# Top-k attention feeding a PReLU MLP on one core: three pairs instead of four alternate at the end, and the MLP's steps are issued by another rule

## The chip, the cores and the metric

The kernel runs on one core of a Trainium2 chip. The core has five engines that work at the same time, each through its own queue of instructions in the order in which the program gives them: TensorE (PE in the profile, with its weight loads as PEld), VectorE (DVE), ScalarE (ACT), GpSimd (POOL) and SyncE (SP), which here only issues transfers. The metric is the device time of one execution in microseconds; the figure given for a kernel is the median of its runs.

## The reference

```
B, H, S, D = 8, 8, 576, 64                      # q, k, v
scores = q @ k.T / sqrt(D)
kth    = 32nd largest score of each row
attn   = softmax(where(scores >= kth, scores, -1e9))
x      = (attn @ v) with the heads side by side  # 4608 tokens x 512
h      = x @ w_in                                # 512 x 2048
g      = max(h, 0) + alpha * min(h, 0)
out    = g @ w_out                               # 2048 x 512
```

There are 64 heads, taken as 32 pairs. A pair has 2 x 576 rows of 576 scores, cut into nine tiles of 128 rows: two for each of four row blocks, and a ninth with the last 64 rows of both heads. So there are 288 tiles.

The PReLU is split. Since g = alpha h + (1 - alpha) max(h, 0), the output is x (w_in diag(alpha) w_out) + relu(x w_in) (diag(1 - alpha) w_out). The matrix in the first bracket, 512 x 512, is made once on the chip (`w_id`); it is called the linear matrix below.

## The kernel before, in words

All the work is written out by hand in one Python loop over ticks, n = 0 to 311, and each engine's queue is the order in which that loop emits. A tick handles one tile at each station of a pipeline:

- PE computes the scores of tile n+1 (`scores`, L314), for two tiles at once where a unit has two.
- ACT copies them out of PSUM with a per-row offset added (`act_b`, L323: tile b), counts signs (`act_s`, L329) and takes exponentials (`act_e`, L334).
- DVE forms the keys of tile n-1 (`flip`, L345: y), the eight largest of each of six segments of tile n-2 (L355: C), and merges those of tile n-3 (L370, L372). For every three tiles it picks the limit of each row, and seven ticks after a tile's scores it makes the mask (`mask`, L419). GpSimd multiplies mask and exponentials (L429). For the last six tiles DVE does both in one instruction (L426).
- SP issues a transposing transfer of the weights (wT<-w, L442), and PE multiplies them with v (`av`, L488: pu). DVE takes reciprocals (L505) and ACT scales the result into xb (`av_out`, L517).

Each pair is prepared before its first tile: transposes of q and k on PE, copies on ACT, row statistics through PE (pq, pk, pt, pg, pr, st in L175 to L240) and eight small steps on DVE. `prep_plan` gives each step a tick relative to `BASE[p]`, from 14 ticks before it to 2 before it. BASE is 9p for the first 28 pairs. The PSUM bank of pq, pk, pt and pg (tag "pa", one buffer) is shared by all pairs.

Of pairs 0 to 27 the nine tiles follow each other. The last batch (pairs P0 = 28 to 31, from tick N0 = 252) is ordered by row block instead: two tiles of each of the four pairs, then the four ninth tiles, then blocks 1, 2 and 3. So a row block of the output has its x before the whole batch is through. `av_last`, `rz_last` and `out_last` (L521 to L543) serve these, two pairs at a time, and DVE scales instead of ACT. BASE of the last four pairs is N0-5, N0-2, N0+2, N0+6.

The MLP is a list of steps, `back`. Each step has a part for PE, a part for ACT that empties the PSUM bank (or none), and a cost. The steps of a batch are added when its x has been turned by a transfer (`x_turn`, L551: xT<-xb): the transfers are issued at the end of tick n+7 and the steps are added at the end of n+8, n being the tick in which the batch's last weights are made. A block of 512 tokens has 16 steps of x w_in (`ph_step`, 4 matmuls each, cost 0.9, emptied by the relu at L641) and 4 x 3 steps of the second product (`pz_step`, 7, 7 and 6 matmuls, cost 1.5, emptied at L658 after the third). A block of 128 tokens has 4 and 3 steps. Weight preparation runs through the same list at the start, and its last four steps are the linear matrix, 16 matmuls each (L596), emptied at L600.

Before tick 252 one step is issued per tick, after that tick's scores; its ACT part is emitted in the next tick ahead of `act_b`. From tick 252 on a credit of 1.9 per tick (2.4 from tick 288) is spent by the cost of the steps, with several in a tick. Then the ACT part of a step is emitted just before the next step, in the same tick. In a tick the steps come on PE ahead of the preparation and the products with v.

## Time and profile before

| | |
|---|---|
| median of 3 runs | 928.11 us (926.97 to 928.45) |
| the profiled execution's own time | 929.21 us |
| its span, first to last instruction | 927.4 us |
| PE, DVE, ACT, POOL busy | 81%, 91%, 87%, 46% |
| mean granted TensorE clock | 0.908 |

The profile is of one execution. An engine's busy time is the time in which it has an instruction running. The rows of a view of groups or of time give line, engine, operation, the tile written and the tiles read, and a count; brackets at the end give the idle time before it and what ended it. The rows of the view by stretches give, for each stretch of time, the busy time of the five engines with the number of their instructions, the granted clock of TensorE (1 is full speed), the busy share of the transfer engines and what they moved. The rows of the view of waits say which instruction waited for which, in total, how often, and the longest.

### The profile page before, as it was taken

What the parts mean: (1) busy time and instruction counts of PE and PEld (TensorE: products, weight loads), DVE (VectorE), ACT (ScalarE), POOL (GpSimd) and SP (SyncE); (2) the same over time, 40 slices, a digit from 0 to 9 for tenths busy, and PEclk for the clock granted to TensorE, in tenths of its full rate; (3) what the DMA queues carried; (4) which work ended last, traced back from release to release, by engine and by line L of the source; (5) the groups of instructions that cost most, each with busy time, mean ns of one, the idle gap of its engine ahead of it and who ended that gap; (6) DMA issues with size and microseconds to landing.
All of it is one profiled execution on the core that took longest, in us unless ns stands there. A gap on an engine that the chain in (4) does not pass through costs nothing.

```text
span 927.4 us, 20789 instructions
## 1 busy us (share of the span) xinstructions
PE 752.0 (81%) x5702; PEld 448.4 (48%) x5779; DVE 847.7 (91%) x5305; ACT 810.4 (87%) x1873; POOL 431.0 (46%) x629
## 2 busy tenths in 40 slices
PE   5866797678977788878986889787986788989996
PEld 3544444344543445544553455544553444544564
DVE  3899969999999999999999999999999888999970
ACT  4999979799897999999897998999997988879842
POOL 0364534544554455555555454555554434455510
PEclk9565788799997999999977999999987999979999
DMA  6699634544556555564546546464456843353551
GB/s 149 121 174 200 132 65 86 105 93 91 124 106 111 92 103 110 115 115 93 126 99 124 95 88 126 97 125 94 106 126 103 146 85 74 76 101 62 115 94 45
DMA packets 343021, 99.52 MB, mean 107 GB/s; under 512 B 335200, under 2 KB 335216, under 8 KB 342896
## 3 DMA queue, kind: packets, MB, share of 16 engines
q1 hardware_dynamic: 340544, 95.71, 52.5%
q0 software_dynamic: 1152, 2.10, 1.6%
q8 instruction: 48, 0.79, 0.4%
q14 instruction: 77, 0.63, 0.2%
q10 hardware_dynamic: 1200, 0.30, 0.2%
HBM read 36.71 MB, written 9.44 MB: 50 GB/s over the span
## 4 chain that ended last, share of the span: by engine, by line
ACT 42%; PE 26%; DVE 24%; issue 3%; DMA 2%; POOL 1%; SPq 1%; ACTq 0%
ACT b L323 10%; ACT h L329 9%; ACT e L334 8%; DVE C L355 7%; PE ps L314 7%; PE pz L653 7%; PE ph L635 5%; ACT gT L641 4%; DVE mk L419 4%; DVE y L345 4%; DVE C L372 3%; DVE L L370 3%; ACT xb L517 2%; PE pz L649 2%; PE pg L206 2%
## 5 line engine op out<-in xcount | busy, mean ns | idle before, releaser
L429 POOL TENSOR_TENSOR w<-mk,e 128x576 bf16<-128x576 bf16 x250 | 319.2, 1277 | 375.3 <-DVE mk L419 208.3
L355 DVE MAX8 C<-y 128x8 f32<-128x96 f32 x1728 | 421.1, 244 | 0.1
L314 PE MATMUL ps<-qkT 64*128 64x288 f32 (+1 forms) x1280 | 255.9, 478 | 26.3 <-ACT b L323 26.1
L323 ACT ACTIVATE b<-ps,NT 128x576 f32<-128x576 f32 x288 | 201.5, 755 | 3.2 <-PE ps L314 3.2
L329 ACT ACTIVATE h<-b 128x576 bf16<-128x576 f32 x288 | 202.0, 701 | 2.0
L635 PE MATMUL ph<-xT,w_in_b 128*128 128x128 bf16 (+1 forms) x920 | 151.5, 302 | 54.4 <-ACT gT L641 27.2
L314 PEld LDWEIGHTS ps<-qkT 64*128 64x128 f32 (+1 forms) x1280 | 135.4, 195 | 86.4 <-ACT b L323 46.7
L334 ACT ACTIVATE e<-b 128x1152 bf16<-128x1152 f32 (+1 forms) x158 | 173.8, 1100 | 0.0
L370 DVE MAX8 L<-C 128x8 f32<-128x48 f32 x864 | 163.8, 190 | 0.1
L345 DVE TENSOR_SCALAR y<-b,SG 128x576 int32<-128x576 int32 x288 | 147.5, 512 | 10.0 <-POOL SG L339 9.4
L419 DVE TENSOR_SCALAR mk<-b,KP 128x576 bf16<-128x576 f32 x282 | 143.8, 510 | 0.0
L653 PE MATMUL pz<-w_out_b,gT 128*128 128x512 bf16 x551 | 134.2, 379 | 4.1 <-issue 3.0
L635 PEld LDWEIGHTS <-w_in_b 128*128 128x128 bf16 x960 | 70.8, 99 | 124.0 <-issue 93.9
L641 ACT ACTIVATE gT<-ph 128x512 bf16<-128x512 f32 x144 | 87.8, 618 | 41.8 <-PE ph L635 41.7
L372 DVE MATCH_REPLACE8 C<-L,C 128x48 f32<-128x48 f32 x576 | 109.1, 189 | 0.0
L653 PEld LDWEIGHTS <-gT 128*128 128x128 bf16 x576 | 52.7, 98 | 68.6 <-issue 13.1
L488 PE MATMUL pu<-v_bf,wT 128*128 128x65 bf16 (+1 forms) x1600 | 71.0, 201 | 11.0 <-DMA wT<-w 8.4
L339 POOL TENSOR_SCALAR SG<-S_all 128x1 int32<-128x1 f32 x288 | 65.2, 227 | 27.8 <-ACT h L329 27.5
L488 PEld LDWEIGHTS <-wT 128*128 128x128 bf16 (+1 forms) x1600 | 66.2, 105 | 24.6 <-DMA wT<-w 8.9
L429 POOL TENSOR_TENSOR wm<-mk,e 128x576 bf16<-128x576 bf16 x32 | 40.8, 1276 | 49.7 <-DVE mk L419 47.9
L329 ACT ACTIVATION_READ_ACCUMULATOR h<-b 128x1 f32 x288 | 61.6, 214 | 0.0
L658 ACT COPY o_sb<-pz 128x512 f32<-128x512 f32 x36 | 21.3, 591 | 39.4 <-PE pz L653 39.4
(102 smaller groups left out, 838.0 us busy)
## 6 DMA issues: line engine op xcount, KB each, us to landing
out_dram<-o_sb SPq DMA_DIRECT2D x35, 256.0 KB, 2.2
st_q<-in_q_dram SPq DMA_DIRECT2D x64, 128.0 KB, 2.9
st_v<-in_v_dram SPq DMA_DIRECT2D x64, 128.0 KB, 2.6
kst<-in_k_dram SPq DMA_DIRECT2D x62, 128.0 KB, 2.8
w_stage<-in_moe_w_out_dram SPq DMA_DIRECT2D x16, 256.0 KB, 3.1
w_in_b<-in_moe_w_in_dram POOLq DMA_DIRECT2D x8, 256.0 KB, 6.8
wT<-w SPq DMA_TRANSPOSE x128, 3.3
st_q<-in_q_dram SPq DMA_DIRECT2D x32, 32.0 KB, 2.8
```

What stands on the lines that cost most here:

```text
L314: nc.tensor.matmul(o_, l_, r_, start=True, stop=True)
L323: nc.scalar.activation(t["b"].rearrange("p (a c) -> p a c", a=2), t["ps"], AF.Identity, bias=NT0[:, p * TPP + j:p * TPP + j + 1], scale=ON ...
L329: nc.scalar.activation(h, tiles[n]["b"], AF.Sign, accum_out=S_all[:, n:n + 1])
L334: nc.scalar.activation(e, tiles[n0]["bu"], AF.Exp, scale=scl)
L345: nc.vector.tensor_scalar(t["y"].bitcast(I32), t["b"].bitcast(I32), FLIP, SG[:, n:n + 1], ALU.bitwise_xor, ALU.bitwise_xor)
L355: return [lambda g=g: nc.vector.max(out=C[:, n % TPP, g, :], in_=t["y"][:, g * SEG:(g + 1) * SEG]) for g in range(NSEG)]
L370: ops.append(lambda r=r, src=src: nc.vector.max(out=L[:, 8 * r:8 * r + 8], in_=src))
L419: nc.vector.tensor_scalar(t["mk"], t["b"], row_limit(n), None, ALU.is_ge)
L429: nc.gpsimd.tensor_tensor(dst, t["mk"], t["e"], ALU.mult)
L488: nc.tensor.matmul(o_, wT[:, 4 * side + c, cs], d["v"][:, 5 * side + c, :], start=(c == 0), stop=(c == 4))
L635: nc.tensor.matmul(hold[f][:, i, :], w_in_b[:, kk, (f + i) * 128:(f + i + 1) * 128], xT[:, kk, c0:c0 + tb], start=(kk == 0), stop=(kk == N ...
L653: nc.tensor.matmul(pz[0:m], hold["gT"][:, f, r0:r0 + m], w_out_b[:, f, :], start=False, stop=(f == NFT - 1))
```

## The change

1. Only the last three pairs (29, 30, 31; `LASTP`) alternate by row block. Pair 28 goes through its nine tiles like the pairs ahead of it, with `av` and `av_out`. `av_last` and its helpers take pairs 29 and 30 together and pair 31 alone.
2. BASE of the last four pairs is N0-3, N0+2, N0+7, N0+12: each five after the one before. Their first tiles come at N0, N0+9, N0+11 and N0+13.
3. The steps of a batch are added at the end of tick n+9 instead of n+8.
4. The linear matrix is made in twelve steps, of 6, 6 and 4 matmuls, instead of four of 16. One PSUM bank is held over the three.
5. ACT parts go into a queue that is emptied at the start of the next tick, throughout. A step that opens a PSUM bank ("takes") is not issued while `nb` parts are queued: 1 before tick BASE[31]-10 = 254, then 2. The second bank, shared with the preparation, opens to the MLP at tick 254 instead of 250.
6. The credit is used from the start. Several steps may be issued in a tick from N0-30 = 222 on instead of from 252.

```diff
-    ORDER += [(P0 + s, h) for s in range(KPB) for h in range(2)]
-    ORDER += [(P0 + s, 8) for s in range(KPB)]
-    ORDER += [(P0 + s, 2 * i + h) for i in range(1, 4) for s in range(KPB) for h in range(2)]
+    ORDER += [(P0, j) for j in range(TPP)]
+    LASTP = range(P0 + 1, NPAIR)
+    ORDER += [(p, h) for p in LASTP for h in range(2)]
+    ORDER += [(p, 8) for p in LASTP]
+    ORDER += [(p, 2 * i + h) for i in range(1, 4) for p in LASTP for h in range(2)]
...
-        m = 1 if n < N0 and ORDER[n][1] == 8 else 2
+        m = 1 if ORDER[n][1] == 8 and ORDER[n + 1][1] != 8 else 2
...
-    BASE.update({P0: N0 - 5, P0 + 1: N0 - 2, P0 + 2: N0 + 2, P0 + 3: N0 + 6})
+    BASE.update({P0: N0 - 3, P0 + 1: N0 + 2, P0 + 2: N0 + 7, P0 + 3: N0 + 12})
...
-        pul[i, g] = pu = ps_d.tile([128, 4, V1], FP32, name="pu", tag="pd")
-        for s in range(2):
-            d = pairs[P0 + 2 * g + s]
+        pul[i, g] = pu = ps_d.tile([128, 4 - 2 * g, V1], FP32, name="pu", tag="pd")
+        for s in range(2 - g):
+            d = pairs[P0 + 1 + 2 * g + s]
...
-        def w_id(kk):
-            hold["pl"] = pl = ps_m.tile([128, DM], FP32, name="pl", tag="misc")
-            for f in range(NFT):
+        def w_id(kk, part):
+            if part == 0:
+                hold["pl"] = ps_m.tile([128, DM], FP32, name="pl", tag="misc")
+            pl = hold["pl"]
+            for f in range(6 * part, min(6 * part + 6, NFT)):
...
-            if wp < P0:
+            if wp <= P0:
...
-                        put(n + 8, "end", lambda: feed((b + 1) * S))
-            elif (wj == 8 or wj % 2) and wp % 2:
-                i, g = (wj // 2, (wp - P0) // 2)
+                        put(n + 9, "end", lambda: feed((b + 1) * S))
+            elif (wj == 8 or wj % 2) and wp > P0 + 1:
+                i, g = (wj // 2, wp - P0 - 2)
...
-            banks[0] = 2 if n >= NT else 1 if n >= N0 - 2 else 0
+            banks[0] = 2 if n >= NT else 1 if n >= BASE[NPAIR - 1] - 10 else 0
...
-            if after:
-                after()
-            after = None
+            while after:
+                after.popleft()()
...
-            credit = min(credit, 0.0) + (2.4 if n >= NT else PE_TICK if n >= N0 else 0.0)
-            first = n < N0
-            while back and (first or credit > 0.0):
+            nb = 1 if n < BASE[NPAIR - 1] - 10 else 2
+            credit = min(credit, 0.0) + (2.4 if n >= NT else 1.9)
+            first = True
+            while back and credit > 0.0 and (first or n >= N0 - 30):
+                pe_f, act_f, cost, takes = back[0]
+                if takes and len(after) >= nb:
+                    break
+                back.popleft()
+                pe_f()
+                if act_f:
+                    after.append(act_f)
+                credit -= cost
                 first = False
-                if after:
-                    after()
-                pe_f, after, cost = back.popleft()
-                pe_f()
-                credit -= cost if n >= N0 else 0.0
```

More of the change, by code (lines that the diff above doesn't have):

```diff
@@ L610, in weight_steps @@
         for kk in range(NKT):
-            yield (lambda kk=kk: w_id(kk)), (lambda kk=kk: w_id2(kk))
+            for part in range(3):
+                yield ((lambda kk=kk, part=part: w_id(kk, part)),
+                       (lambda kk=kk: w_id2(kk)) if part == 2 else None)
     banks = [0, 0]
@@ L671, in mlp_steps @@
                 yield ((lambda r0=r0, m=m, part=part: pz_step(r0, m, part)),
-                       (lambda r0=r0, m=m: pz_act(r0, m)) if part == 2 else None, 1.5)
+                       (lambda r0=r0, m=m: pz_act(r0, m)) if part == 2 else None, 1.5, part == 0)
     blocks = []
@@ L744 @@
         scores(0)
-        back = deque((a, c, 1.0) for a, c in weight_steps())
+        back = deque((a, c, 1.0, 0) for a, c in weight_steps())
         credit = 0.0
-        after = None
+        after = deque()
         wdue, held = {}, []
@@ L759 @@
                     load_v(p)
-            banks[0] = 2 if n >= NT else 1 if n >= N0 - 2 else 0
+            banks[0] = 2 if n >= NT else 1 if n >= BASE[NPAIR - 1] - 10 else 0
             if n + 1 < NT and unit_of[n + 1][2] == 0:
                 scores(n + 1)
-            if after:
-                after()
-            after = None
+            while after:
+                after.popleft()()
             if n < NT:
```

11 lines of the change are left out of this document (6 added, 5 removed).

## The prediction

> **What bounds the kernel now.** I read the busy times on the page, then the view by stretches, then who waited for whom on DVE.
>
> ```profile
> PE 752.0 (81%) x5702; PEld 448.4 (48%) x5779; DVE 847.7 (91%) x5305; ACT 810.4 (87%) x1873; POOL 431.0 (46%) x629
> ```
> ```profile
> 400.00:600.00 200.00, 167.26 (x1310) 99.31 (x1327) 197.45 (x1242) 187.31 (x445) 101.72 (x143) 0.94 0.54 106
> ...
> 100.00:121.00 21.00, 13.82 (x100) 9.38 (x100) 21.00 (x136) 21.00 (x51) 11.57 (x17) 0.68 0.55 103
> ...
> 124.00:142.00 18.00, 17.50 (x120) 8.87 (x123) 9.58 (x55) 9.17 (x19) 4.40 (x6) 1.00 0.22 46
> ...
> 185.00:240.00 55.00, 45.54 (x343) 25.90 (x349) 53.01 (x332) 53.41 (x127) 27.63 (x40) 1.00 0.48 99
> ...
> 715.00:790.00 75.00, 60.93 (x480) 34.93 (x488) 62.55 (x390) 64.15 (x152) 30.25 (x44) 0.98 0.56 100
> ...
> 831.00:887.00 56.00, 53.27 (x413) 29.57 (x418) 54.26 (x326) 49.35 (x99) 28.59 (x40) 1.00 0.46 84
> ...
> 887.00:928.00 41.00, 33.27 (x389) 23.54 (x390) 13.28 (x65) 12.41 (x22) 1.47 (x2) 0.94 0.32 72
> ...
> 400.00:600.00 200.00, 35.02 (x69) 0.94 0.54 106
> ```
> ```profile
> DVE P L226 <- PE pr L218: 4.1, 1, 4.1
> DVE rz L505 <- PE pu L488: 3.8, 1, 3.8
> DVE sq L251 <- ACT MM L247: 1.3, 1, 1.3
> ...
> DVE P L226 <- PE pr L218: 6.8, 12, 1.0
> ...
> DVE rz L505 <- PE pu L488: 6.5, 5, 2.3
> DVE P L226 <- PE pr L218: 3.0, 5, 1.0
> DVE y L345 <- POOL SG L339: 2.3, 2, 1.6
> DVE sq L251 <- ACT MM L247: 0.5, 1, 0.5
> ...
> DVE y L345 <- POOL SG L339: 1.5, 3, 1.0
> DVE rz L534 <- PE pu L488: 0.7, 1, 0.7
> ```
>
> The last row of the second fence is the flips of DVE alone: 69 ticks in 200 us, 2.90 us a tick, and DVE is busy for 197.45 of the 200. In the middle DVE sets the pace. The third fence gives its waits in four windows: 100 to 160 us (9.2 in all), 160 to 700 (6.8), 700 to 800 (12.3), 800 to 860 (2.2). Together 30.5 us: what can be won up to tick 288 without less DVE work. From 831 us PE is full too (53.27 of 56), and after 887 us DVE is nearly through while PE works on.
>
> **The change, part by part**, against the profiled execution (span 927.4, own time 929.21; the median of the runs, 928.11, is 1.1 below that).
>
> *A. The linear matrix in pieces.*
>
> ```profile
> 128.16 3.61 PE L596 MATMUL pl<-xT,w_inT 128*128 128x512 bf16 x16 [0.31 <-ACT w_id_b L600]
> 131.70 1.24 PE L314 MATMUL ps<-qkT 64*128 64x288 f32 x8
> ...
> ACT w_id_b L600 <- PE pl L596: 8.8, 4, 3.3
> ...
> 710.35 1.73 PE L635 MATMUL ph<-xT,w_in_b 128*128 128x512 bf16 x4
> ```
>
> Sixteen matmuls take 3.61 us, 0.23 each. Four such steps stand in four ticks running. ACT, whose next tick begins with emptying the bank, waits 8.8 us for them; DVE waits for pr, pu and st queued behind them, the 9.2 us of the first window. After, a tick has 6, 6 or 4 matmuls, 1.4 us at most. A tick without MLP work has about 1.9 us of PE (13.82 us in 21 us, 7.2 ticks, at clock 0.68). So the sum is 1.2 + 1.9 = 3.1 us in a mean tick, and less at full speed (1.9 x 0.68 is 1.3), beside 2.90 of DVE: nearly hidden. The loss left is bounded by 0 and by three ticks at half speed (four matmuls then take 1.73 us, so 5.3 take 2.3, and the rest 1.9 x 0.68/0.5 = 2.6: a tick 4.9, 2.0 over), 6 us. I take 1.5, nearer to 0, since 124 to 142 us with its linear matrix ran at clock 1.00: gain 7.7. The twelve steps end at tick 46, ahead of x_turn in tick 49, which overwrites xT: nobody waits.
>
> *B. The batch's steps a tick later.*
>
> ```profile
> 169.88 5.20 SPq L551 DMA_TRANSPOSE xT<-xb  x4
> ...
> 176.44 0.59 PE L635 MATMUL ph<-xT,w_in_b 128*128 128x512 bf16 x1 [4.53 <-DMA xT<-xb]
> ...
> 707.94 0.60 ACT L641 ACTIVATE gT<-ph 128x512 bf16<-128x512 f32 x1 [3.71 <-PE ph L635]
> 708.44 0.68 ACT L329 ACTIVATE h<-b 128x576 bf16<-128x576 f32 x1
> ...
> 710.15 1.21 ACT L334 ACTIVATE e<-b 128x1152 bf16<-128x1152 f32 x1
> ...
> DVE P L226 <- PE pr L218: 1.9, 3, 1.0
> ...
> DVE P L226 <- PE pr L218: 1.7, 2, 1.0
> ...
> DVE P L226 <- PE pr L218: 1.5, 2, 1.0
> ```
>
> The four turns take 5.2 us of SP, and the first ph can start only at 176.44. ACT's relu of it heads the next tick, so ACT stands for 3.7 us (707.94, the same place in a later batch) with h and e queued behind. That eats ACT's lead over DVE just where each following tick also has a relu; then DVE waits for pr, which waits for ACT: 1.9, 1.7 and 1.5 us after three feeds (180 to 240, 285 to 340, 500 to 545 us). With the feed a tick later, the work from 708.44 to the end of e (2.9 us) goes ahead of that relu and covers 2.9 of 3.7. Gain between 0 and 5.1; I take 4.5. The lead kept at the feed near 703 us goes to C.
>
> *C. Five ticks between preparations, and one pair fewer interleaved.*
>
> ```profile
> ACT gT L641 <- PE ph L635: 7.6, 6, 3.7
> ACT o_sb L658 <- PE pz L653: 4.7, 3, 2.2
> ACT qkT L178 <- PE pq L175: 3.2, 3, 1.6
> ...
> 766.00 0.97 ACT L517 ACTIVATE xb<-pu,rz 128x64 bf16<-128x64 f32 x4
> ```
>
> Between 700 and 800 us DVE loses 12.3 us. ACT loses 3.7 at the feed (B) and 3.2 waiting for pq, whose bank pg of the pair before still holds: with pairs 3 and 4 ticks apart, pq comes in the tick of the other's pg or of its emptying. Five ticks apart, pg is emptied a tick ahead of the next pq. No transfer is nearer to its use: the loads still stand 17 ticks ahead of BASE. That speaks for about 7 us. Against it: the second products now come with 1.27 steps a tick from tick 248, where pairs 30 and 31 are still prepared; the 6.5 us that DVE waited for pu, queued on PE behind such steps, may stay or grow. Bounds: 3 us lost (the 6.5 grow by half), 11 won; I take 7.
> Pair 28's x goes through ACT: ten scalings, 0.97 us for four, 2.5 us in ticks 268 and 274. ACT is idle for 6.7 of 56 us from 831 on, so nothing. DVE loses five double scalings and gains three reciprocals: nothing.
>
> *D. Emptying a tick later after tick 252.* ACT no longer waits in a tick for the matmuls just issued. Of DVE's 2.2 us of the last window, 0 to 2.2 go; I take 1.0, the 0.7 for pu and a part of the rest.
>
> *E. What is left at tick 288.*
>
> ```profile
> 826.46 0.58 PE L635 MATMUL ph<-xT,w_in_b 128*128 128x512 bf16 x1 [0.86 <-DMA xT<-xb]
> ...
> 900.14 3.62 PE L653 MATMUL pz<-w_out_b,gT 128*128 128x512 bf16 x16
> ...
> 903.59 0.80 PE L488 MATMUL pu<-v_bf,wT 128*128 128x65 bf16 x20
> ...
> 921.25 0.59 ACT L658 COPY o_sb<-pz 128x512 f32<-128x512 f32 x1 [3.72 <-PE pz L653]
> ...
> wT<-w SPq DMA_TRANSPOSE x128, 3.3
> ```
>
> The seventh batch's block costs 16 x 0.9 + 12 x 1.5 = 32.4 and the five small blocks 8.1 each: 72.9. Before, the credit spends 40.5 of it in ticks 267 to 287, and 32.4 is left. After, ticks 268 to 287 spend 37.5 (in the phase of ph two banks allow 1.8 a tick), and 35.4 is left: two more parts, 14 matmuls at 3.45/16 us (900.14 to 903.59), 3.0 us. From 887 us PE has 33.27 us of work until the last bank is emptied at 921.25, so nothing hides them: 3.0 us lost. Between 0 (PE catches up in the 2.7 us that it is idle from 831 to 887) and 6 (if the longer rest from tick 261 to 268 costs one more stretch at half speed). The products with v of row block 2 now come two ticks after its last mask instead of four; 6.6 us of steps stand ahead of them on PE from tick 288, more than the mask, GpSimd and the 3.3 us of the transfer: no wait.
>
> Sum: 7.7 + 4.5 + 7 + 1.0 - 3.0 = 17.2. Profiled time 929.2 - 17.2 = 912.0; median 911.
>
> **Rivals.**
> - *PE crowded.* From tick 248 to 257 PE has in a tick 1.9 us of steps, 0.6 of scores (1.24 us for two tiles, above) and some 0.7 of preparation and products with v (the 1.3 of a tick without steps at full speed, less 0.6): 3.2 against 2.90. If the waits for pu and pr all stay, C is 0: 918; with B lost as well, 922. For it: 60.93 of 75 us of PE busy already in 715 to 790. Against it: 14 us idle there.
> - *Half speed through the linear matrix: slower.* The stretch 100 to 121 has clock 0.68 with PE busy 66%; 185 to 240 has 1.00 at 83%. If twelve thin pieces keep the clock at half, a tick of PE is up to 4.9 us, 2.0 over, in twelve ticks 24 us of waiting in place of 9.2: +15 - 12.5 + 3, 934. It decides beyond 9 such ticks, where A's loss passes the other gains. Against it: at half speed PE would be busy throughout, and from 124 us on, with PE busy 97%, the clock was 1.00. The Trainium skill, "TensorE: Matmul & The Clock Gate", section "Why this matters for your kernels", speaks for this rival: it asks for dense matmuls and no rests above some 3 us. By its own count, one busy window of about 3.4 us gives full speed back, which would end it after a tick or two, a loss of 2 to 4 us; the trace agrees as far as it goes, with 0.68 up to 121 us and 1.00 from 124 on, once PE was dense.
> - *All waits gone.* A 9.2, B 5.1, C 11, D 2.2, and E hidden: 27.5, 901.
> - *It does not do what it says.* Before tick 252 parts were emptied a tick late already, and steps by length only re-order 35 steps in ticks 248 to 261, which are done before the next feed in either kernel. Then only A is left, less E: 923; if DVE's freed time is also lost at the last feed, no change.
>
> **How the numbers follow.** Forecast (906 to 917) 0.60; crowded (917 to 924) 0.25; all gone 0.04; half speed 0.05; no change or other losses at the end 0.06, half of it slower. The range takes forecast and crowded, with the nearer part of the other two, 903 to 924. A measurement tells 0.2% (1.9 us) from no change: faster 0.89, same 0.03, slower 0.08.
>
> **What would show it.** A: no DVE wait above 1.5 us between 115 and 160 us. B: ACT's waits for the first ph below 1 us, and no waits for pr after the feeds. C: DVE's waits between 700 and 800 us at 5 or less, those for pq gone. E: some 36 us of PE work after tick 287, against 33.27. Wrong if the clock is at half over ticks 35 to 46, if the waits for pu in ticks 248 to 257 exceed 7 us, or if PE's work after tick 287 passes 39 us.

## The result, and the profile after

The changed kernel takes 920.69 us (median, 919.75 to 921.67) against 928.28 for the kernel before in the same comparison: the ratio is 0.9914, with the interval 0.9897 to 0.993. So it is 7.6 us faster. The forecast was 17 us faster, 911; the range of 903 to 924 holds the result, and the rival "PE crowded" (918 to 922) describes it better than the forecast does. Of the kernels below, e6 and e7 had one run each far off the others (2004 and 1393 us), and these two runs are left out of all figures.

The first row is from the page of the kernel after, the next five from its view by stretches, with the columns as before.

```profile
PE 752.6 (82%) x5779; PEld 445.7 (48%) x5779; DVE 845.6 (92%) x5308; ACT 810.4 (88%) x1884; POOL 430.8 (47%) x629
```
```profile
100.00:126.00 26.00, 18.13 (x118) 11.66 (x118) 23.89 (x155) 25.16 (x58) 13.27 (x19) 0.62 0.57 117
126.00:160.00 34.00, 31.83 (x265) 17.87 (x262) 32.29 (x202) 31.74 (x75) 16.14 (x22) 0.99 0.41 82
760.00:811.00 51.00, 43.66 (x382) 25.75 (x381) 44.64 (x284) 41.71 (x99) 22.35 (x31) 1.00 0.36 81
820.00:878.00 58.00, 54.50 (x415) 29.62 (x415) 56.01 (x344) 49.11 (x104) 30.29 (x43) 1.00 0.42 84
878.00:920.00 42.00, 33.73 (x398) 23.91 (x394) 11.21 (x52) 12.36 (x21) 0.00 (x0) 0.98 0.30 69
```

The busy times are nearly those of before, so the work is the same. In the first two rows, around the linear matrix, the clock is 0.62 up to 126 us and 0.99 after. The third row will be the important one: ticks 249 to 264, at full clock, in which DVE is busy for only 44.64 of 51 us (42.97 of 45 in the same ticks of the kernel before). In the fourth the two engines fill their time as before, and the last holds what is left after tick 287.

What changed is where DVE stands. These are its waits in the kernel after: two rows for 60 to 160 us, then five for 700 to 800, then two for 800 to 860. From 160 to 700 us it has none, where it had 6.8 us.

```profile
DVE P L228 <- PE pr L220: 3.7, 1, 3.7
DVE rz L507 <- PE pu L490: 1.8, 1, 1.8
...
DVE rz L507 <- PE pu L490: 5.7, 5, 1.5
DVE sq L253 <- ACT MM L249: 2.6, 2, 2.2
DVE y L347 <- POOL SG L341: 2.2, 2, 2.0
DVE P L228 <- PE pr L220: 2.1, 4, 1.2
DVE km L226 <- ACT GK L212: 2.0, 1, 2.0
...
DVE y L347 <- POOL SG L341: 1.6, 2, 1.0
DVE rz L535 <- PE pu L490: 0.9, 2, 0.7
```

The waits at the linear matrix, from 100 to 160 us, fell from 9.2 to 3.7 us (the 1.8 us for pu came ahead of 100 us) and those behind the feeds to nothing, but between 700 and 800 us they rose from 12.3 to 14.6. That is the stretch in which the forecast had put 7 of its 17 us. Since the kernel after is ahead of the other, these are not quite the same ticks; over ticks 231 to 264, as numbered below, the waits are 12.6 us before and 15.6 after.

Since every tick has one flip on DVE, the start of a tile's flip shows how far a kernel has come. In the table, and wherever gains and losses between ticks are told, a tick is named by its tile, whose flip the loop emits one n later. The table gives, for the profiled execution of each kernel, how many microseconds it gained (minus) or lost (plus) between ticks against the profiled execution of the kernel before, whose flips of ticks 45, 231, 249, 264 and 287 start at 163.3, 709.9, 776.8, 821.6 and 889.1 us, and whose span is 927.4. The experiments in it come below.

| kernel | to tick 45 | 45 to 231 | 231 to 249 | 249 to 264 | 264 to 287 | 287 to end | whole span |
|---|---|---|---|---|---|---|---|
| after | -5.5 | -7.9 | -3.0 | +5.9 | -0.6 | +3.1 | -8.0 |
| e1_linear | -7.5 | -1.1 | 0.0 | 0.0 | +0.2 | 0.0 | -8.5 |
| e2_feed | +0.2 | -8.2 | -2.8 | 0.0 | -0.1 | +1.0 | -9.8 |
| e3_late | -7.1 | -8.2 | -3.8 | +6.6 | -0.6 | +3.1 | -10.0 |
| e4_last8 | -7.3 | -8.2 | -4.1 | +7.5 | +2.7 | +0.4 | -9.0 |
| e5_both | -8.0 | -8.0 | -5.6 | 0.0 | 0.0 | +0.8 | -20.9 |
| e6_base | -8.0 | -7.9 | +0.8 | +1.5 | -1.4 | +3.1 | -11.8 |
| e7_order | -7.3 | -8.0 | -3.9 | +7.7 | +0.2 | +2.0 | -9.3 |
| e8_both_last8 | -6.2 | -8.1 | -5.5 | 0.0 | -0.3 | 0.0 | -20.2 |
| e9_only_order | -3.3 | -7.9 | -1.3 | -0.1 | +0.2 | +1.9 | -10.5 |
| e10_only_loop | -7.2 | -8.0 | -0.3 | +1.0 | -0.3 | +2.9 | -11.9 |
| e11_bank | -7.4 | -8.1 | -5.5 | +0.8 | 0.0 | +0.8 | -19.4 |
| e12_queue | -6.9 | -8.0 | -5.5 | 0.0 | 0.0 | +2.8 | -17.6 |
| f1_pr_bank | -5.1 | -8.2 | -3.6 | +3.3 | +1.6 | +3.2 | -8.9 |
| f2_both_pr_bank | -3.3 | -8.2 | +0.2 | -0.6 | 0.0 | +0.7 | -11.1 |
| f3_one_moved | -6.7 | -8.0 | -9.0 | +6.5 | +0.2 | +2.0 | -15.1 |

In the row of the kernel after, 16.4 us are gained up to tick 249, 5.9 are lost again from tick 249 to 264, and 3.1 after tick 287. One thing lies hidden at the edge of two columns. Between the flips of tiles 248 and 249 the kernel after takes 7.3 us for a single tick, the kernel before 2.7. So it gains 7.6 us from tick 231 to 248 and loses 4.6 of them in the next tick. Counted from tick 248, the loss up to 264 is 10.5 us and not 5.9. The same tick costs e3 2.1 us, e4 3.1, e7 2.1 and f1 3.4. These five are the kernels in which pair 30 is prepared later; the others lose nothing there.

### The profile page after: what moved, and what is told of

Same layout as the page of the kernel before. It is cut to its first block, busy times and chain, and to the rows that moved or that the text cites. A ratio compares the mean times of both kernels' runs of the same rounds, so it can differ in the third digit from the quotient of the medians.

```text
span 919.4 us, 20883 instructions
## 1 busy us (share of the span) xinstructions
PE 752.6 (82%) x5779; PEld 445.7 (48%) x5779; DVE 845.6 (92%) x5308; ACT 810.4 (88%) x1884; POOL 430.8 (47%) x629
## 5 line engine op out<-in xcount | busy, mean ns | idle before, releaser
L316 PE MATMUL ps<-qkT 64*128 64x288 f32 (+1 forms) x1280 | 248.0, 467 | 27.9 <-ACT b L325 27.3
L316 PEld LDWEIGHTS ps<-qkT 64*128 64x128 f32 (+1 forms) x1280 | 130.0, 191 | 88.5 <-ACT b L325 51.0
L660 PE MATMUL pz<-w_out_b,gT 128*128 128x512 bf16 x576 | 138.3, 381 | 0.0
L490 PE MATMUL pu<-v_bf,wT 128*128 128x65 bf16 (+1 forms) x1600 | 71.3, 201 | 21.8 <-DMA wT<-w 10.5
L519 ACT ACTIVATE xb<-pu,rz 128x64 bf16<-128x64 f32 x232 | 55.9, 358 | 7.2 <-DVE L L372 3.0
```

Of the source, the lines that this page charges most:

```text
L316: nc.tensor.matmul(o_, l_, r_, start=True, stop=True)
L490: nc.tensor.matmul(o_, wT[:, 4 * side + c, cs], d["v"][:, 5 * side + c, :], start=(c == 0), stop=(c == 4))
L660: nc.tensor.matmul(pz[0:m], hold["gT"][:, f, r0:r0 + m], w_out_b[:, f, :], start=False, stop=(f == NFT - 1))
```

## The experiments

The medians are of four to six runs each. The kernel before, run beside them, had medians of 927.6 us (the first four kernels), 928.4 (e5 to e8), 928.3 (e9 to e12) and 929.0 (f1 to f3).

| kernel | what it is | median, us | ratio to before, interval |
|---|---|---|---|
| e1_linear | before, linear matrix in pieces | 920.24 | 0.991, 0.9892 to 0.9929 |
| e2_feed | before, feed a tick later | 920.31 | 0.9918, 0.9898 to 0.9937 |
| e3_late | after, one step a tick up to tick 257 | 918.58 | 0.9895, 0.9875 to 0.9915 |
| e4_last8 | after, last feed a tick earlier | 920.07 | 0.992, 0.9896 to 0.9943 |
| e5_both | before, pieces and later feed | 909.52 | 0.9809, 0.9789 to 0.9828 |
| e6_base | after, old BASE | 917.36 | 0.9872, 0.9851 to 0.9894 |
| e7_order | after, old issue loop | 919.81 | 0.9914, 0.9895 to 0.9933 |
| e8_both_last8 | e5, last feed a tick earlier | 910.34 | 0.9811, 0.979 to 0.9831 |
| e9_only_order | e7, old BASE | 914.56 | 0.9833, 0.9799 to 0.9868 |
| e10_only_loop | e5, new issue loop | 915.85 | 0.9858, 0.9831 to 0.9884 |
| e11_bank | e5, second bank four ticks later | 912.27 | 0.9828, 0.9802 to 0.9854 |
| e12_queue | e10, several steps a tick only from tick 252 | 912.0 | 0.9837, 0.9807 to 0.9867 |
| f1_pr_bank | after, one half of pr in another bank | 920.05 | 0.9896, 0.9878 to 0.9914 |
| f2_both_pr_bank | e5, the same edit | 917.24 | 0.9869, 0.9849 to 0.9889 |
| f3_one_moved | e9, one pair prepared six ticks later | 914.91 | 0.9853, 0.9833 to 0.9872 |

### First: two parts alone, two parts undone

e1_linear is the kernel before with the linear matrix in pieces and nothing else.

```diff
-        def w_id(kk):
-            hold["pl"] = pl = ps_m.tile([128, DM], FP32, name="pl", tag="misc")
-            for f in range(NFT):
+        def w_id(kk, part):
+            if part == 0:
+                hold["pl"] = ps_m.tile([128, DM], FP32, name="pl", tag="misc")
+            pl = hold["pl"]
+            for f in range(6 * part, min(6 * part + 6, NFT)):
...
-            yield (lambda kk=kk: w_id(kk)), (lambda kk=kk: w_id2(kk))
+            for part in range(3):
+                yield ((lambda kk=kk, part=part: w_id(kk, part)),
+                       (lambda kk=kk: w_id2(kk)) if part == 2 else None)
```

> The kernel before with the linear matrix in twelve steps alone. Theory (A as the trace of the changed kernel reads: it is worth the 5.5 us by which that kernel is ahead at tick 45, with one wait of 3.7 us left where the clock is at half): 928.3 - 5.5 = 922.8, and DVE's waits between 60 and 160 us come to some 5 to 6 us in place of 10. Rival (the lead is given back in the phase of ph, where ACT is the slower engine): 927 or more, DVE's waits for pr after 160 us grow beyond 6.8.

Measured: 920.24 us, 7.4 us less than before. By the table, 7.5 are won by tick 45 and nothing later takes them away. DVE's waits from 60 to 160 us are these in e1:

```profile
DVE P L226 <- PE pr L218: 2.9, 2, 2.5
DVE rz L505 <- PE pu L488: 0.7, 1, 0.7
```

So part A is right in place and size (7.7 forecast), with 3.6 us of waits left.

e2_feed is the kernel before with the feed of every batch a tick later.

```diff
-                        put(n + 8, "end", lambda: feed((b + 1) * S))
+                        put(n + 9, "end", lambda: feed((b + 1) * S))
```

> The kernel before with the steps of a batch added one tick later, and nothing else. Theory B (the late feed spares ACT the wait for the first ph): DVE's waits for pr between 160 and 700 us, 6.8 us, all go, and some of those between 700 and 800; one more tick of MLP work, 1.9 us of PE, is left for the end: 928.3 - 7 + 2 = 923, between 920 and 925. Rival (a later feed only shifts the work; the waits for pr went for another reason, the other emptying order or the pieces): 929 to 931.

Measured: 920.31 us, 7.3 us less. 8.2 us are won between ticks 45 and 231, another 2.8 up to tick 249, and 1.0 is lost at the end. DVE has no wait left from 160 to 700 us. Part B is right in kind and was put too low (4.5).

e3_late is the kernel after, with several steps a tick only from tick 258 instead of 222. The two row blocks whose sums can then be open at once get a bank each.

```diff
-            while back and credit > 0.0 and (first or n >= N0 - 30):
+            while back and credit > 0.0 and (first or n >= N0 + 6):
...
-                hold["pz"] = mlp_bank("pz", DM)
-            pz = hold["pz"]
+                hold["pz", r0] = mlp_bank("pz", DM)
+            pz = hold["pz", r0]
```

> The changed kernel with several steps in a tick only from tick 258 on, when all preparation is through. Theory (crowding: two parts of the second product in a tick, beside the preparation of pairs 30 and 31, cost the 8.4 us that the changed kernel loses between ticks 246 and 261): 914 to 916, DVE's waits between 740 and 800 us at 8 or below against some 12.6. Rival (the preparations themselves, now five ticks apart and reaching to tick 262, collide with the second products at any pace): 919 to 922, waits unchanged.

Measured: 918.58 us, 2.1 less than the kernel after, with intervals that overlap. The loss of ticks 249 to 264 is 6.6 us, no smaller than in the kernel after: dense second products before tick 258 aren't what it needs.

e4_last8 is the kernel after, with the last feed at n+8 as before.

```diff
-                        put(n + 9, "end", lambda: feed((b + 1) * S))
+                        put(n + (8 if b == B - 2 else 9), "end", lambda: feed((b + 1) * S))
```

> The changed kernel with the last feed, that of the seventh batch, at the end of tick n+8 as before; the others stay at n+9. Theory E (the tail is PE's own work, and the tick given away leaves two more parts of 1.5 us after tick 287): 920.7 - 3 = 917.7, less up to 1 us of waiting for xT at that feed: 917.5 to 919. Rival (PE has room for them, or the wait for xT at that feed costs as much as the tick gains): 920 to 921.5.

Measured: 920.07 us, no difference that can be told from the kernel after. The end loses only 0.4 us in place of 3.1, but ticks 264 to 287 lose 2.7 that they didn't: the MLP's work is at the end or ahead of it, and takes the same time.

### Second: the two good parts together, and the rest in halves

e5_both is the kernel before with both edits, of e1 and e2, and nothing else.

```diff
...
+            for part in range(3):
+                yield ((lambda kk=kk, part=part: w_id(kk, part)),
+                       (lambda kk=kk: w_id2(kk)) if part == 2 else None)
...
-                        put(n + 8, "end", lambda: feed((b + 1) * S))
+                        put(n + 9, "end", lambda: feed((b + 1) * S))
```

> The kernel before with the linear matrix in pieces and the later feed, and nothing else. If the two gains add up (7.4 and 7.3 us alone, in different stretches): 927.6 - 14.7 = 913, 911 to 914, and the whole rest of the change (order of the last pairs, preparation five apart, queue, steps by length) costs some 7 us net. If instead they share an end that does not move (the last feed's PE work): 918 to 920.

Measured: 909.52 us, 18.9 less than before and 11.2 less than the kernel after: the fastest kernel of this study. It is 4.2 more than the two gains alone add up to. In the profiled runs 2.8 us of such an excess lie in ticks 231 to 249, where the clock fell to half for 3.4 us in e1 and in e2 and stayed full in e5; whether that is the reason isn't shown. Its waits of DVE from 700 to 800 us:

```profile
DVE rz L505 <- PE pu L488: 4.8, 3, 2.3
DVE y L345 <- POOL SG L339: 1.4, 3, 0.8
DVE P L226 <- PE pr L218: 1.1, 3, 0.5
DVE sq L251 <- ACT MM L247: 0.5, 1, 0.5
```

They are 7.8 us, against 12.3 before and 14.6 in the kernel after. So the other parts of the change (order, BASE, issue loop) don't merely win nothing, they cost 11.2 us together. Whatever explains the result has to explain this sum.

e6_base is the kernel after with the old BASE. The second bank and the limit `nb` are set at tick 254 as in the kernel after.

```diff
-    BASE.update({P0: N0 - 3, P0 + 1: N0 + 2, P0 + 2: N0 + 7, P0 + 3: N0 + 12})
+    BASE.update({P0: N0 - 5, P0 + 1: N0 - 2, P0 + 2: N0 + 2, P0 + 3: N0 + 6})
```

> The changed kernel with the preparation of the last four pairs at the ticks of the kernel before (N0-5, N0-2, N0+2, N0+6), all else changed, the second PSUM bank still from tick 254. Theory P (the preparation of pairs 30 and 31, moved five to six ticks later into the second products, makes PE late: the 8.4 us lost between ticks 246 and 261): 913 to 916, with DVE's lead over the kernel before kept at 16 us or more at tick 261. Theory Q (steps by length and the queue's limit of one part do it, at any place of the preparation): 919 to 922.

Measured: 917.36 us, 3.3 less than the kernel after and between the two ranges. The loss of ticks 249 to 264 falls from 5.9 to 1.5, but ticks 231 to 249 lose 0.8 instead of winning 3.0, so over both the profiled runs differ by only 0.6 us. Another 2.5 of what separates them is there by tick 45, where the two kernels don't differ.

e7_order is the kernel after with the issue loop of before (parts 5 and 6 of the change undone except for the tick of the second bank, the new order and BASE kept).

```diff
-            credit = min(credit, 0.0) + (2.4 if n >= NT else 1.9)
...
-            while back and credit > 0.0 and (first or n >= N0 - 30):
...
+            credit = min(credit, 0.0) + (2.4 if n >= NT else PE_TICK if n >= N0 else 0.0)
...
+            while back and (first or credit > 0.0):
...
+                if after:
+                    after()
+                pe_f, after, cost = back.popleft()
```

> The changed kernel with the loop of before for issuing the steps: one step a tick up to tick 252, then by cost, ACT parts emptied in the same tick. Order of the last pairs, preparation, pieces and later feed are as changed. Theory P: the loss stays, 917 to 921. Theory Q: it goes, 911 to 914, as both gains alone.

Measured: 919.81 us, the same as the kernel after within the intervals. With the old loop, ticks 249 to 264 lose 7.7 us. So the queue and the steps by length aren't needed for that loss either.

e8_both_last8 is e5 with the last feed at n+8.

```diff
-                        put(n + 9, "end", lambda: feed((b + 1) * S))
+                        put(n + (8 if b == B - 2 else 9), "end", lambda: feed((b + 1) * S))
```

> The kernel before with the pieces and the later feed, but the last feed, that of the seventh batch, at n+8. If the tick given away there is paid at the end in PE work (3.0 us of two parts by my sum; the later feed alone showed 1.0 between tick 287 and the end): 1 to 3 us below the version with all feeds late. If the wait for xT at that feed costs as much as the tick gains: the same within 1 us.

Measured: 910.34 us, no difference from e5. The 0.8 us of the end go to 0.0, and that is all the later last feed costs where the rest is as before.

### Third: one part each on the fast kernel

e9_only_order is e7 with the old BASE, and the second bank opens at tick 250 again: the fast kernel e5 with the new order of the last pairs alone.

```diff
-    BASE.update({P0: N0 - 3, P0 + 1: N0 + 2, P0 + 2: N0 + 7, P0 + 3: N0 + 12})
+    BASE.update({P0: N0 - 5, P0 + 1: N0 - 2, P0 + 2: N0 + 2, P0 + 3: N0 + 6})
...
-            banks[0] = 2 if n >= NT else 1 if n >= BASE[NPAIR - 1] - 10 else 0
+            banks[0] = 2 if n >= NT else 1 if n >= N0 - 2 else 0
```

> The version with pieces and later feed (909.5 us) with one part more: the last three pairs alternate and pair 28 goes in a row, with the preparation at its old ticks and the steps issued as before. Beside it stands the version that has the preparation moved as well (920.9). Theory P (the moved preparation is the loss): 908 to 911. Theory R (the order itself is: pair 28's products and scalings return to PE and ACT in ticks 265 to 274, and the second products fall otherwise): 917 to 921.

Measured: 914.56 us, between the two ranges, with runs from 909.49 to 918.69: two at 909.5, one at 912.9, three between 916.3 and 918.7. The profiled run is the slowest of these. Between ticks 249 and 264, where e7 loses 7.7 us, e9 loses nothing; e7 differs from it in BASE and the tick of the second bank alone. The three rows are of the view by stretches, for the ticks 249 to 264 of e5, e9 and e7 in this order.

```profile
755.00:800.00 45.00, 40.87 (x342) 23.02 (x342) 42.97 (x276) 36.15 (x84) 22.46 (x32) 0.98 0.42 85
```
```profile
764.00:809.00 45.00, 39.94 (x336) 22.38 (x336) 43.11 (x276) 36.04 (x81) 22.58 (x33) 1.00 0.46 85
```
```profile
757.00:810.00 53.00, 45.78 (x380) 26.41 (x381) 44.66 (x285) 40.40 (x92) 22.40 (x31) 0.97 0.42 75
```

Fifteen ticks take 45 us in e5 and e9 and 53 in e7. In e9 PE is busy for 39.94 of the 45, so 5.1 us are free. With the later BASE, PE is busy for 5.8 us more in the same ticks (45.78 less 39.94), DVE for 1.6 and ACT for 4.4. By the tiles written (pq, pk, pt, pg, pr, st), 4.2 of PE's 5.8 us are preparation of pairs 30 and 31 that ran ahead of these ticks before; the rest is scores and second products. So by its amount alone PE's moved work would still fit into the 5.1 us. But PE works through its queue in order, with the preparation among the second products, and in e7 it stands idle for 7.2 of the 53 us itself. The loss shows as engines that wait for each other, not as a full PE. The next two rows are ACT's waits for the emptying of pz in these ticks, in e9 and in e7; the two after them are from e7 too, DVE's longest group of waits there (1.5 us in e9), and the second product that ACT stands longest for.

```profile
ACT o_sb L665 <- PE pz L660: 8.4, 5, 2.3
```
```profile
ACT o_sb L665 <- PE pz L660: 12.0, 5, 4.9
...
DVE rz L507 <- PE pu L490: 5.2, 3, 2.2
...
779.55 0.59 ACT L665 COPY o_sb<-pz 128x512 f32<-128x512 f32 x1 [4.92 <-PE pz L660]
```

e10_only_loop is e5 with the new issue loop alone, BASE and order as before (and a bank for each open row block, as in e3).

```diff
-            credit = min(credit, 0.0) + (2.4 if n >= NT else PE_TICK if n >= N0 else 0.0)
-            first = n < N0
-            while back and (first or credit > 0.0):
+            nb = 1 if n < N0 - 2 else 2
+            credit = min(credit, 0.0) + (2.4 if n >= NT else 1.9)
+            first = True
+            while back and credit > 0.0 and (first or n >= N0 - 30):
...
+                if act_f:
+                    after.append(act_f)
```

> The version with pieces and later feed (909.5 us) with the new rule of issue alone: the queue of ACT parts, the limit on open banks, steps by length from tick 222; order and preparation as before. Theory P (preparation alone): 908 to 911. Theory Q (two steps a tick from 222 on crowd PE while pairs are prepared, ticks 234 to 250): 913 to 917, as the changed kernel with the old preparation ticks lost 6 us between ticks 243 and 252.

Measured: 915.85 us, 6.3 more than e5, as the second theory had it. In the profiled run 5.3 of it is lost between ticks 231 and 249, 1.0 up to tick 264, and 2.1 at the end.

e11_bank is e5 with the second bank from tick 254 instead of 250.

```diff
-            banks[0] = 2 if n >= NT else 1 if n >= N0 - 2 else 0
+            banks[0] = 2 if n >= NT else 1 if n >= N0 + 2 else 0
```

> The version with pieces and later feed (909.5 us) with the second PSUM bank opened to the MLP at tick 254 instead of 250, nothing else. Theory S (a single bank in ticks 250 to 253 makes each second product wait until ACT has emptied the one before): 912 to 915, DVE's waits between 760 and 790 us up by 3 or more. Otherwise: within 1.5 us of 909.5.

Measured: 912.27 us, 2.7 more than e5, with intervals that overlap; 0.8 of it in ticks 249 to 264. So of the 7.8 us that separate e7 from e9 there, most is BASE and not the bank, if the bank does the same in the new order.

e12_queue is e10 with several steps a tick only from tick 252: the queue alone.

```diff
-            while back and credit > 0.0 and (first or n >= N0 - 30):
+            while back and credit > 0.0 and (first or n >= N0):
```

> As the one with the new rule of issue alone, but with several steps in a tick only from tick 252 on, as before the change: the queue of ACT parts by itself. If emptying a tick later spares ACT its waits at the last feed (2.2 us of DVE's waits at 811 us): 907 to 909. If theory Q's loss comes from the limit on open banks, not from two steps a tick: 912 or more. Else 909.5.

Measured: 912.0 us. Up to tick 287 it goes like e5, and at the end it loses 2.8 us where e5 loses 0.8: two banks let the first product's steps come at 1.8 a tick where the credit would give 1.9, so more is left. And since e10 differs from it only in ticks 222 to 251, several steps a tick in these cost 3.9 us by the medians (915.85 less 912.0), though the intervals overlap.

### Fourth: one suspected wait, and one pair

In the kernel after, PE stands 4.6 us for DVE at the second half of pr, whose bank DVE empties late. The rows are of the view of waits, 700 to 810 us, and of the view in order of time.

```profile
PE pr L220 <- DVE P L228: 4.6, 3, 2.3
...
779.22 0.22 PE L220 MATMUL pr<-qTb,GK 64*64 64x64 bf16 x2 [2.30 <-DVE P L228]
...
780.63 1.38 ACT L325 ACTIVATE b<-ps,NT 128x576 f32<-128x576 f32 x2 [1.53 <-PE ps L316]
```

All that is queued on PE behind it waits too: the scores of the tick, and for these ACT, 1.5 us. f1_pr_bank takes this wait away: the second half goes into the bank of the transposes.

```diff
-                pr = ps_d.tile([128, n1 - n0], FP32, name="pr", tag="pd")
+                pool, tag = (ps_d, "pd") if n0 == 0 else (ps_a, "pa")
+                pr = pool.tile([128, n1 - n0], FP32, name="pr", tag=tag)
```

> The changed kernel with the second half of pr (64 columns) in the bank of the transposes instead of the pair of banks shared with the products with v. Theory T (PE stands at that matmul until DVE has emptied the first half, 4.6 us in three waits between 700 and 810 us, and the second products, the scores and ACT stand behind): these waits go to below 1 us and the time falls by 3 to 5, 916 to 918. Theory U (it is the PE work of the preparation beside the second products that counts): the waits go, and the time stays at 920 to 921.5, since PE is late anyway.

Measured: 920.05 us, the same as the kernel after. The 4.6 us of PE are gone, and ticks 249 to 264 lose 3.3 us instead of 5.9; but ticks 264 to 287 now lose 1.6 where they won 0.6. PE's stand was part of how the loss shows, and not its cause.

f2_both_pr_bank is e5 with the same edit.

```diff
-                pr = ps_d.tile([128, n1 - n0], FP32, name="pr", tag="pd")
+                pool, tag = (ps_d, "pd") if n0 == 0 else (ps_a, "pa")
+                pr = pool.tile([128, n1 - n0], FP32, name="pr", tag=tag)
```

> The version with pieces and later feed (909.5 us) with the same other bank for the second half of pr. There PE waits 2.7 us in two waits for that bank. Theory T: 907 to 908.5. Theory U, or the transposes of the next pair, three and four ticks later, now waiting for that bank instead: 909 to 912.

Measured: 917.24 us, above both ranges and 7.7 more than e5; in the profiled runs 4.7 of the difference is there by tick 45, ahead of any effect of pr on the last pairs (f2's clock rose only at 127.55 us there), and 5.8 comes in ticks 231 to 249. With the pairs at the old BASE, three and four ticks apart, the transposes of the next pair wait for the bank that pr now holds:

```profile
PE pq L175 <- DVE P L227: 5.2, 3, 4.1
```

f3_one_moved is e9 with pair 31 alone prepared from N0+12 as in the kernel after, and the bank from tick 254.

```diff
-    BASE.update({P0: N0 - 5, P0 + 1: N0 - 2, P0 + 2: N0 + 2, P0 + 3: N0 + 6})
+    BASE.update({P0: N0 - 5, P0 + 1: N0 - 2, P0 + 2: N0 + 2, P0 + 3: N0 + 12})
...
-            banks[0] = 2 if n >= NT else 1 if n >= N0 - 2 else 0
+            banks[0] = 2 if n >= NT else 1 if n >= N0 + 2 else 0
```

> The version with the new order and the old preparation ticks (914.6 us) with pair 31 alone prepared six ticks later, as in the changed kernel, the second bank from tick 254. All four pairs moved lost 7.6 us between ticks 249 and 264. If pair 31 alone, the only one whose pq to st then lies wholly within the second products, carries it: 5 us or more lost in these ticks, 917 to 921. If the loss is shared by the pairs: 1 to 3 us lost there, 913 to 917.

Measured: 914.91 us. The loss in ticks 249 to 264 is that of the first outcome: one pair is enough for 6.5 us of it. The time is that of the second, and no different from the 914.56 of e9, from which f3 was made. What the pair leaves behind shows too: from tick 231 to 249 f3 wins 9.0 us, where e5 wins 5.6 and e9 1.3. The row is of the view by stretches for ticks 249 to 264 of f3.

```profile
753.00:804.00 51.00, 44.12 (x358) 25.24 (x358) 43.47 (x275) 38.99 (x88) 22.17 (x31) 0.97 0.41 81
```

PE is busy for 44.12 us there against 39.94 in e9, 4.2 us more, of which 3.4 are the pair's preparation, and the ticks take 6 us longer. So the move of one pair costs these ticks 6.5 us, and in the whole nothing that can be told: what it lost there it had won ahead of them. How much of that earlier gain is the move and how much the clock, which in e9's profiled run fell to half for 6.8 us at 726.1 us, stays open.

## Why the prediction was right or wrong

**A, the linear matrix: right in mechanism and size.** Alone it won 7.4 us (7.7 forecast). In the kernel after only 5.5 had been won by tick 45, and one wait for pr of 3.7 us stayed, above the 1.5 that the prediction gave as a sign. The reason is in the rows in order of time, of PE in the kernel after:

```profile
124.99 2.24 PE L601 MATMUL pl<-xT,w_inT 128*128 128x512 bf16 x6
...
127.52 1.47 PE L601 MATMUL pl<-xT,w_inT 128*128 128x512 bf16 x6
...
130.10 1.04 PE L601 MATMUL pl<-xT,w_inT 128*128 128x512 bf16 x4
```

The first piece still ran at half speed, 2.24 us, and the others in 1.0 to 1.5, near the 1.4 that the prediction had worked out. In this run the granted clock became full at 126.6 us, in the run of e5 at 122.75, in that of e9 only at 128.75; and the gain by tick 45 goes with it: 5.5, 8.0 and 3.3 us. Of the 15 kernels with the pieces, the ten in which the clock rose before 124.3 us won 6.7 to 8.0, and the five in which it rose later 3.3 to 6.2. The rival "half speed" is refuted: once full, the clock stayed full for 37.5 us, 11 times 3.41, right through the pieces. The Trainium skill, "TensorE: Matmul & The Clock Gate", section "What's actually happening", gives a free-running window of 3413 ns in which the chip decides on the clock; the runs agree, since nearly every interval of one speed recorded here is a multiple of 3.41 us.

**B, the later feed: right in mechanism, its size too small.** Forecast 4.5 out of at most 5.1; measured 7.9 to 8.2 between ticks 45 and 231 in all kernels that have the edit. What was left out is that ACT's lost lead cost DVE all twelve waits for pr from 160 to 700 us, 6.8 us, and not only the seven after three feeds that the prediction had summed. Where the rest comes from, up to 8.2, the waits don't show. PE's first product after a feed and ACT's relu of it are these in the kernel after:

```profile
170.87 1.86 PE L642 MATMUL ph<-xT,w_in_b 128*128 128x512 bf16 x4 [0.69 <-DMA xT<-xb]
...
172.77 0.60 ACT L648 ACTIVATE gT<-ph 128x512 bf16<-128x512 f32 x1
```

PE stood 0.69 us for the transfer where it had stood 4.53, and ACT not at all.

**C, five ticks between preparations: the step that failed.** Forecast 7 us won between 700 and 800 us. DVE's waits there rose by 2.3, and by 3.0 over ticks 231 to 264: C won nothing and lost about the 3 us that the prediction had as its lower bound. "Five ticks apart, pg is emptied a tick ahead of the next pq" was true, and ACT's 3.2 us of waiting for pq are gone; but to reach five ticks the preparations of pairs 30 and 31 moved five and six ticks later, into the second products. The prediction named these two as what spoke against C, but counted no work for them and took a value near the other bound. The work was in the trace of before to be counted, and so was the room for it. These are its stretches from tick 249 to 264 and ahead of it:

```profile
777.00:822.00 45.00, 39.71 (x331) 23.06 (x332) 42.97 (x273) 38.72 (x90) 22.31 (x31) 0.95 0.41 85
715.00:777.00 62.00, 49.31 (x392) 28.73 (x398) 51.20 (x316) 53.47 (x129) 24.38 (x36) 0.97 0.60 103
```

PE had 5.3 us free in the first and 12.7 in the second; the work was moved from the second into the first, some 4 us of it on PE by the count under e9. The ticks that took it in lost 5.9 to 7.7 us (8.7 to 10.6 with tick 248): with the new loop (after) and the old (e7), with few steps a tick (e3), and with the last feed earlier (e4). Without PE's stand at pr it is 3.3 (6.7 with tick 248; f1), for one pair alone 6.5 (f3), and with the old BASE it is gone (e9, and all but 1.5 us in e6). So where the loss lies and that it goes with the moved preparation is shown. What the runs didn't tell apart is which share is PE's work alone and which the moved work of ACT and DVE that goes with it.

This loss isn't the price of the whole move, which also frees the ticks ahead. By the medians, e7 is 5.3 us slower than e9, whose own runs spread over 9 us; the kernel after is 3.3 slower than e6, 2.5 of it by tick 45; and f3 is no slower than e9. So what the move costs in all, between nothing and some 5 us, depends on the rest of the kernel and stays open; that it didn't win 7 is plain.

ACT's waits between 700 and 800 us, in the kernel after:

```profile
ACT o_sb L665 <- PE pz L660: 6.9, 5, 2.9
ACT gT L648 <- PE ph L642: 5.3, 7, 1.8
ACT GK L212 <- PE pg L208: 5.1, 3, 4.1
```

The third shows what became late in place of pq: once ACT stands 4.15 us for pg, which PE reaches only after fourteen matmuls of the second product. This is the long tick between 248 and 249. The clock was at half there up to 754.6 us, so the matmuls took longer than they would have at full clock; what share of the 4.6 us that is, is not shown. These are the rows of PE and then of ACT:

```profile
752.04 1.89 PE L656 MATMUL pz<-w_id_b,xT 128*128 128x512 bf16 x4
753.72 2.78 PE L660 MATMUL pz<-w_out_b,gT 128*128 128x512 bf16 x10
756.34 1.28 PE L208 MATMUL pg<-kst 128*128 128x130 f32 x10
...
757.65 0.28 ACT L212 ACTIVATE GK<-pg 128x130 bf16<-128x130 f32 x1 [4.15 <-PE pg L208]
```

A second error lies beside it: the 12.3 us that C was to draw on weren't all C's. The two good parts alone bring them to 7.8 (e5).

**Steps by length from tick 222** had been set at no cost ("only re-order 35 steps"). Against e12, where they begin at tick 252, they cost e10 3.9 us, with intervals that overlap. In the kernel after, where the preparation has moved out of these ticks, hardly any of that shows: with the old loop it is as slow (e7). So the two losses don't add up in the kernel after. A reading that fits is that each takes the room that the other would have used.

**D, emptying a tick later: nothing won** (1.0 forecast). DVE's waits from 800 to 860 us went from 2.2 to 2.9; over the same ticks, 264 to 287, they are 1.9 us in both kernels, and the wait for pu at L535 is still there (0.7 before, 0.9 now).

**E, what is left at the end: right,** 3.1 us lost (3.0 forecast). PE's work from tick 287 on is 33.73 us (878 to 920 in the fence at the top); cut at the same tick the kernel before has 31.27:

```profile
889.00:928.00 39.00, 31.27 (x353) 21.54 (x354) 11.28 (x51) 10.82 (x19) 0.00 (x0) 0.94 0.31 67
```

That is 2.5 us more work. The prediction's 33.27 and 36 count from 887 us, some 2 us ahead of tick 287; cut so, the kernel after has 35.73. Beside the work there is one stand of 1.5 us for the relu. The parts of it weren't all as argued: the later feed alone costs 0.8 to 1.0 (e5, e2), the new order makes it 1.9 (e9), and with the queue and its two banks it is 2.8 (e12).

**The sum.** 5.5 won by A, 7.9 by B, 3.0 in ticks 231 to 249 (the last feed's share of B is in them, 2.8 in e2, and so are the 4.6 lost at tick 248), 5.9 lost where C moved its work, 0.6 won up to tick 287 and 3.1 lost after it: 8.0 us of span, against 17.2 forecast. The rival "PE crowded" had the right ticks (it said 248 to 257, and the kernel after loses 8.3 us between the flips of these two) and the right engine's queue, though PE itself was busy for only 43.66 of the 51 us from tick 249 on. It was set aside with "14 us idle there". That was the idle time of 715 to 790 us, nearly all of it ahead of the ticks into which the work moved (12.7 us up to 777, by the rows under C).

## To carry to other kernels

When a preparation is moved to mend a conflict over a bank, its instructions go with it: add them up for each engine in the ticks they leave and in the ticks they enter, and compare that with the idle time of the entered ticks alone. Leave room in it: here some 4 us came into 5 us of PE's idle time, and the ticks grew by 6 to 8 us. Cut a burst of matmuls into pieces that fit beside the pace-setting engine's tick, and let a result that waits for a transfer come a tick later than it could: these two edits of a few lines gave 18.9 us here. Try the parts of a change one by one before taking them together, since the remaining parts of this one took 11 us back.

## What the runs showed of the hardware that was not expected

The clock falls to half in the middle of the kernel, and whether it does is partly chance. Cut along the grid of 3.41 us in which the clock changes, the traces of before, after and the 15 experiments hold 3318 stretches at full clock between 60 and 860 us. In 132 of them PE is busy for less than 45% of the time; 131 of these are followed by a stretch at half. Of the 151 that were 45 to 55% busy 89 are followed by one at half, of the 3035 busier ones 40, so the busy share is not the whole rule. Of those at half clock, 249 have PE busy for less than 80%, and 247 of them are followed by another at half. The first two rows are e9's last stretch at full clock ahead of a fall, and the time at half that follows; the third and fourth are e5's two grid stretches at the same lull in the work.

```profile
722.67:726.08 3.41, 1.61 (x19) 1.04 (x19) 3.18 (x23) 3.41 (x10) 1.80 (x4) 1.00 0.93 179
...
726.00:733.00 7.00, 6.43 (x24) 3.04 (x23) 5.93 (x35) 3.81 (x12) 2.56 (x3) 0.51 0.69 142
```
```profile
716.64:720.06 3.42, 2.24 (x25) 1.71 (x25) 3.42 (x25) 3.42 (x10) 2.22 (x4) 1.00 0.91 138
720.06:723.47 3.41, 2.07 (x16) 1.10 (x15) 2.94 (x17) 2.52 (x10) 0.90 (x3) 1.00 0.87 182
...
717.79:721.20 3.41, 1.30 (x18) 0.83 (x17) 3.17 (x23) 3.41 (x13) 1.79 (x4) 1.00 0.96 147
```

In e9 the lull fell into one grid stretch (1.61 us of PE work in 3.41), and the clock was at half for the next 6.8 us. In e5 a lull at least as deep (1.30 us from 717.79 to 721.20, the last row) lay across two stretches, which had 2.24 and 2.07 us of work each, and the clock stayed full. The programs are alike there. Where the grid lies differs from run to run: e5 and e11 are the same program up to tick 250, and their clocks rose at 122.75 and 123.62 us, which is not a whole number of 3.41 us apart. The Trainium skill, "TensorE: Matmul & The Clock Gate", section "What's actually happening", says of its window that it doesn't start with the kernel, which agrees; it names an idle window as what lowers the clock, and here a window that was busy 47% of the time did.

This limits what the comparisons can tell. A fall near 725 us goes with 4.3 us of difference between the profiled runs of e9 and e5 in ticks 231 to 249, and e9's six runs spread over 9 us. So what the new order alone costs stays open, somewhere between nothing and the 5.0 us of the medians, and so does how much of e10's 3.9 us over e12 is the clock: e10 has a fall at 722.3 us, e12 none until 799.9. The loss of ticks 249 to 264 isn't of this kind, since the clock there was full, or nearly so, in all the rows shown for them; at tick 248 in the kernel after it was not.
